# Gate and up of three row blocks in 64-row pairs on TensorE's own semaphore, two spectra kept, a third weight buffer

## The chip, the cores and the metric

The kernel runs on one NeuronCore of one Trainium2 chip. The metric is the device time of one execution in microseconds. Five engines take part: TensorE (PE; its weight loads are listed apart as PEld), VectorE (DVE), ScalarE (ACT), GpSimd (POOL) and SyncE (SP), which issues nearly all transfers. Each works through its own queue in order; semaphores tie the queues together.

## The reference

One transformer layer on 2048 rows of 576 channels: a long convolution with a gate, then a gated feed-forward part, each behind a layernorm that a condition vector scales and shifts.

```python
sa, ca, ga, sb, cb, gb = six rows of (silu(c) @ w_mod)
h = layernorm(x) * (1 + ca) + sa
kv = (4-tap causal shift of k by shift_k) * v
y = causal convolution of kv with ssm_k over 2048 steps (by FFT, per channel) + kv * ssm_D
x = x + ga * (h * y)
h = layernorm(x) * (1 + cb) + sb
x = x + gb * ((silu(h @ w1) * (h @ w3)) @ w2)        # w1, w3: 576 x 4608, w2: 4608 x 576
```

Inputs and output are bf16.

## The kernel before

**Two strands of work.** The feed-forward part runs over four row blocks `r` of 512 rows (`RB`). For each, *gate and up* computes 36 hidden tiles `f` of 128 columns of `h @ w1` and `h @ w3`, and `down` (L1043) multiplies the hidden 512 x 4608 block by `w2` in two column halves of nine chunks each. Beside it runs the convolution of the next two 256-row blocks `s0`, `s1`, written as a Python generator (`conv`, L822) whose steps each state a cost. After every hidden tile, `hide` (L964) calls `advance` (L903), which adds an allowance to `due` and takes steps until their costs have used it up. The allowance is `rate * 2.05`, times `HEAD_PACE` (1.8) for the first eight tiles of `r` > 0; `down` gives one per chunk. So a convolution step's matmuls enter TensorE's queue among those of the feed-forward part. On the other engines a compile-time scheduler orders what is ready by program order; `behind` and `issue_after` fix an order by hand. In `down`, after six chunks of the second half, `end` takes all steps left, and `turn_all` (L793) transposes the last rows for the next row block.

**The convolution.** Block `s` of `k*v` and of the filter become spectra `X[s]` and `V[s]` (six 128 x 576 planes each). `forward2` (L310) makes one with four pairs of 288-column matmuls into PSUM and a ScalarE copy of each. `pair` (L408) multiplies an X with a V and adds to the block's sum `z`: two DVE instructions over 3456 elements. `inverse` (L544) transforms `z` back. Three X and four V fit in SBUF; the others are written to DRAM (`keep_x`, `keep_v`) and read again (`get`, L440). `outcome` (L751) does the steps from `z` to the normalised rows `h2row`; `ln_sums` (L448) takes two ScalarE passes for a layernorm's sums. `k_rows` (L363) transposes the filter rows.

**Gate and up.** A hidden tile contracts 576 channels: four 128-row tiles and one of 64 rows. Its gate and up sums fill the two banks of one of four PSUM buffers (`ps`, L72). For `r` < 3, `stream` (L914) takes two tiles at a time: 128-row matmuls (`full`, L943), then the 64-row remainders (`rest`, L954), gate on array rows 0 to 63 and up on rows 64 to 127, then 128-row matmuls again. For `r` = 3, `stream_halves` (L1004) uses 64-row matmuls alone. They come in pairs on the upper and lower array rows, one into each bank: five pairs (`part(f, 0)`), then four (`part(f, 1)`) with the banks swapped. [...] A one-element POOL memset on `tok` waits for the first part's last matmul, and the swapped part's first matmul waits for the memset:

```python
for f in range(NF + 1):
    if f < NF:
        ...
        part(f, 0)
    if f > 0:
        part(f - 1, 1)
        hide(f - 1)
```

The 36 tiles' weights come in nine jobs of four tiles. `load_w13` (L894) puts 1152 KB into one of the buffers `wst[0]`, `wst[1]` by turns. `wst[2]` is the same memory as `w2m`, which holds four chunks of `w2` for `down`.

Of the kernel before, what the change touches and what calls it, by code (L numbers as in the profile page):

```python
# [33 lines left out]
SPLIT = 2  # L34
HEAD = 8
HEAD_PACE = 1.8
# [10 lines left out]
class _Kernel:  # L47
    def __init__(self, ctx, tc, q, k, v, shift_k, ssm_k, ssm_D, w1, w3, w2, c, w_mod, out):
# [21 lines left out]
        self.gets = 0  # L70

# [4 lines left out]
    def setup(self):  # L76
# [3 lines left out]
        self.tok = const.tile([1, 1], F32, name="tok")  # L80
# [215 lines left out]
    def forward(self, basis, rhs, dst):  # L296

        nc = self.nc
        for e in range(2):
            for cs in range(2):  # L300
                ps = self.ps()
                for cc in range(2):
                    for h in range(2):
                        nc.tensor.matmul(ps[:, h, 0:H], basis[:, cc * (e + 1), cs],
                                         rhs[:, cc, h * H:(h + 1) * H],
                                         start=(cc == 0), stop=(cc == 1))
                nc.scalar.copy(dst(e, cs).rearrange("p (h d) -> p h d", h=2), ps[:, :, 0:H])
                yield -1.0

    def forward2(self, basis, rhs, both, odd, diff):  # L310
# [3 lines left out]
        for cc, dst in ((0, both), (1, odd)):  # L314
            for cs in range(2):
                ps = self.ps()
                for h in range(2):
                    nc.tensor.matmul(ps[:, h, 0:H], basis[:, cc, cs], rhs[:, cc, h * H:(h + 1) * H],  # L318
                                     start=True, stop=True)
                nc.scalar.copy(dst[:, cs].rearrange("p (h d) -> p h d", h=2), ps[:, :, 0:H])  # L320
                yield -1.9
# [34 lines left out]
    def x_sums(self, s):  # L356
        X = self.X[s]
        self.nc.vector.tensor_add(X[:, 0:6:3, :], X[:, 1:6:3, :], X[:, 2:6:3, :])
        if 3 < s < NBLK - 2:
            self.keep_x(s)  # L360
        yield 0.75

    def k_rows(self, s):  # L363
# [5 lines left out]
        for cc in range(2):  # L369
            for ct in range(5):  # L370
                nc.tensor.transpose(pt[:, cc, ct * P:(ct + 1) * P], nat[:, ct, cc:B:2],
                                    self.ident[:])
        nc.scalar.copy(kT[:], pt[:, :, 0:D])
# [59 lines left out]
    def old_x(self, i, s):  # L433

        return self.X[i] if s == 2 or s == 4 and i > 0 else self.get("X", i)
# [12 lines left out]
    def ln_sums(self, src, i, ssum, ssq, col=None):  # L448
        col = i if col is None else col
        for func, scale, out in ((ACT.Copy, -1.0 / D, ssum), (ACT.Square, D ** -0.5, ssq)):  # L450
            junk = self.lnp.tile([P, D], BF16, name="junk", tag="junk")
            self.nc.scalar.activation(junk[:], src[:, i, :], func, scale=scale, accum_out=out[:, col:col + 1])  # L452
# [40 lines left out]
    def gate_stats(self, s):  # L493

        ssum, ssq = [self.small.tile([P, 2], F32, name="l1" + k, tag=t) for k, t in (("s", "ssum"), ("q", "ssq"))]
        for i in range(2):
            with self.behind(self.nc.scalar):
                self.ln_sums(self.xo[s], i, ssum, ssq)
            yield 0.8
# [44 lines left out]
    def inverse(self, s, cc):  # L544
        nc = self.nc
        z = self.accs[s]
        ps = self.ps()
# [4 lines left out]
        for i, (b, cs, row) in enumerate(terms):  # L552
            for h in range(2):
                nc.tensor.matmul(ps[:, h, 0:H], self.Fb[:, b, cs], z[:, row, h * H:(h + 1) * H],
                                 start=(i == 0), stop=(i == len(terms) - 1))
        return ps
# [27 lines left out]
    def turn(self, pt, cc):  # L584
        for ct in range(5):
            self.nc.tensor.transpose(pt[:, cc, ct * P:(ct + 1) * P],  # L586
                                     self.h2row[:, cc, ct * P:(ct + 1) * P], self.ident[:])
# [20 lines left out]
    def turned(self, s, pt, c0, n):  # L608
# [4 lines left out]
        for ct in range(5):  # L613
            dst = hT[:, ct, t * P:(t + n) * P].rearrange("p (c t) -> p c t", c=n)
            src = pt[:, c0:c0 + n, ct * P:(ct + 1) * P]
# [27 lines left out]
    def first_block(self):  # L643
# [54 lines left out]
        self.ln_sums(x1, 0, sums[0], sums[1], 0)  # L698
# [7 lines left out]
        ps = [self.inverse(0, cc) for cc in range(2)]  # L706
# [44 lines left out]
    def outcome(self, s, fill, waits, between=None, quick=False):  # L751


        def steps():
# [4 lines left out]
            for cc in range(2):  # L759
                nc.scalar.copy(y[:, cc, :].rearrange("p (h d) -> p h d", h=2), self.inverse(s, cc)[:, :, 0:H])  # L760
# [13 lines left out]
            else:  # L774
                sums = [self.small.tile([P, 2], F32, name="l2" + k, tag=t) for k, t in (("s", "ssum"), ("q", "ssq"))]
                for i in range(2):
                    with self.behind(nc.scalar):
                        self.ln_sums(self.xo[s], i, *sums)
                    yield 0.0
# [42 lines left out]
    def conv(self, s0):  # L822
# [13 lines left out]
        def old():  # L836
            V, X = self.old_v(s0 - 1, s0), self.old_x(1, s0)
            yield from self.pair(X, V, s0, s0 == 2)
            for j in range(2, s0):
                X = self.old_x(j, s0)  # L840
                yield from self.pair(X, V, s1)
                V = self.old_v(s0 - j, s0)
                yield from self.pair(X, V, s0)
            self.V1 = V
# [8 lines left out]
        def beside():  # L853
# [7 lines left out]
            self.X1 = self.old_x(1, s0)  # L861
# [12 lines left out]
        def others():  # L874
            yield from self.kv_rows(s1)
            self.gate_shift(s1)
            yield from self.mix(self.x_spectrum(s1), more())
            yield from self.x_sums(s1)
        yield from self.outcome(s0, others(), (5.0, 4.5, 6.0, 0.0), lambda: self.gate_rows(s1))
# [23 lines left out]
    def advance(self, cost):  # L903

        self.due += cost
        while self.due > 0 and self.steps is not None:
            c = next(self.steps, None)
            if c is None:
                self.steps = None
                break  # L910
            self.due -= c
# [85 lines left out]
    def wait_for(self, later, first):  # L997

        self.tc.add_manual_dep(
            later, first.name,  # L1000
            mybir.DependencyInfo(mybir.DependencyClass.Sync, mybir.DependencyReason.DATA),
            reason="both halves of the rows write this bank, one after the other")

    def stream_halves(self, r):  # L1004
# [3 lines left out]
        newest = lambda: nc.cur_bb.bb.instructions[-1]  # L1008
        gus, ws, marks = {}, {}, {}

        def part(f, swap):
            w = ws[f // FC]
            cols = slice(f % FC * P, (f % FC + 1) * P)
            for ct in range(4 if swap else 5):
                for rows, i in ((slice(0, 64), swap), (slice(64, P), 1 - swap)):
                    nc.tensor.matmul(gus[f][:, i, :], w[rows, 5 * i + ct if ct < 4 else 4, cols], hT[rows, ct, :],  # L1016
# [180 lines left out]
```

## Time and profile before

| what | us |
|---|---|
| median of 3 runs (519.62 to 520.41) | 520.09 |
| the profiled execution | 519.61 |
| its span, first to last instruction | 517.8 |
| `r` = 0 with the start, to 171.6 | 171.6 |
| `r` = 1: gate and up / down | 82.8 / 37.8 |
| `r` = 2: gate and up / down | 79.1 / 37.3 |
| `r` = 3: gate and up / down and end | 70.1 / 39.1 |
| PE / DVE / ACT busy | 498.4 / 345.5 / 292.9 |

The stage borders are read from the chain of work that ended last. The profile page lists busy time by engine, the chain, groups of instructions with the idle time before them and what ended it, and transfers. A timeline gives instructions in order of time. The end of a matmul is modelled, so its starts are the safer reading.

### The profile page before, as it was taken

The page shows a single profiled execution, that of the slowest core. Times are in us where ns is not written, and L with a number is a line of the kernel's source. Part 1 is how long each engine was busy: PE and PEld are TensorE (multiplying, and loading weights), DVE is VectorE, ACT ScalarE, POOL GpSimd, SP SyncE. Part 2 cuts the span into 40 slices and gives each one's busy share as a digit, 9 for nine tenths or more (in the row PEclk, how much of TensorE's full clock was granted, in tenths as well). Part 3 has the DMA queues.
Part 4 walks back from the last instruction along what each step waited for, and adds up shares of the span by engine and source line. Part 5 has one row for each costly group of instructions (what it writes and reads, how often), then busy time and mean ns, then how long its engine had stood idle before and what let it go on. Part 6 is the DMA issues. An engine that isn't in the chain of part 4 may idle for free.

```text
span 517.8 us, 9255 instructions
## 1 busy us (share of the span) xinstructions
PE 498.4 (96%) x3650; PEld 294.8 (57%) x3650; DVE 345.5 (67%) x557; ACT 292.9 (57%) x581; POOL 26.1 (5%) x75
## 2 busy tenths in 40 slices
PE   7999989889989999899999999999999999999997
PEld 3667765456868544343677644434587644444775
DVE  8888799999997287989999637998711222221012
ACT  5748689649254488577641467958651355555000
POOL 3100000000000001000001000000100000000000
PEclk9999999989999999999999999999999999999999
DMA  8947959646998696688788549653655535532462
GB/s 262 331 151 210 308 178 289 203 143 221 315 342 270 207 312 230 214 284 289 230 270 280 161 147 361 200 173 91 184 147 151 161 107 176 175 110 77 117 181 69
DMA packets 102207, 107.80 MB, mean 208 GB/s; under 512 B 5075, under 2 KB 94228, under 8 KB 102164
## 3 DMA queue, kind: packets, MB, share of 16 engines
q1 hardware_dynamic: 102142, 107.21, 66.5%
q8 instruction: 28, 0.46, 0.4%
q14 instruction: 15, 0.12, 0.1%
q10 hardware_dynamic: 22, 0.01, 0.0%
HBM read 96.00 MB, written 11.21 MB: 207 GB/s over the span
## 4 chain that ended last, share of the span: by engine, by line
PE 70%; DVE 20%; DMA 4%; ACT 3%; issue 2%; POOL 1%; SPq 0%; DVEq 0%; POOLq 0%; ACTq 0%
PE ps L949 24%; PE ps L1061 22%; PE ps L1016 14%; PE ps L960 4%; DVE p L420 3%; DMA wst<-in_B_w_dram 3%; DVE z L422 3%; DVE h L971 2%; PE ps L318 2%; DVE z L414 1%; DVE kv L342 1%; DVE kvt L341 1%; PE ps L253 1%; DMA knat<-in_A_ssm_k_dram 1%; ACT junk L452 1%
## 5 line engine op out<-in xcount | busy, mean ns | idle before, releaser
L949 PE MATMUL ps<-h2T,wst 128*128 128x512 bf16 (+1 forms) x1056 | 201.1, 341 | 1.9 <-DMA wst<-in_B_w_dram 0.9
L949 PEld LDWEIGHTS <-wst 128*128 128x128 bf16 x1056 | 100.3, 98 | 87.7 <-issue 14.8
L1061 PE MATMUL ps<-wst,h 128*128 128x288 bf16 x1152 | 145.1, 286 | 2.4 <-DVE og L1078 1.4
L1061 PEld LDWEIGHTS <-h 128*128 128x128 bf16 x1152 | 112.3, 98 | 32.0 <-issue 3.1
L968 ACT ACTIVATE h<-ps 128x512 bf16<-128x512 f32 x108 | 65.2, 603 | 64.7 <-PE ps L960 40.8
L1016 PE MATMUL ps<-h2T,wst 64*128 64x512 bf16 x648 | 70.1, 376 | 0.0
L970 ACT CAST u<-ps 128x512 bf16<-128x512 f32 x108 | 63.7, 590 | 0.0
L971 DVE TENSOR_TENSOR h<-h,u 128x512 bf16<-128x512 bf16 x108 | 44.5, 417 | 24.6 <-ACT u L970 24.6
L420 DVE TENSOR_TENSOR p<-X,V 128x3456 bf16<-128x3456 bf16 x28 | 54.6, 1951 | 2.0 <-DMA X<-Xd 1.8
L422 DVE TENSOR_TENSOR z<-z,p 128x3456 bf16<-128x3456 bf16 x28 | 54.6, 1950 | 0.2
L1016 PEld LDWEIGHTS <-wst 64*128 64x128 bf16 x648 | 31.5, 94 | 38.4 <-DMA wst<-in_B_w_dram 0.4
L1031 DVE TENSOR_TENSOR h<-h,u 128x512 bf16<-128x512 bf16 x36 | 15.3, 425 | 54.9 <-ACT u L1030 54.9
L1078 DVE TENSOR_TENSOR og<-ps,gbrow 128x288 bf16<-128x288 f32 x32 | 13.1, 449 | 50.5 <-PE ps L1061 50.5
L1028 ACT ACTIVATE h<-ps 128x512 bf16<-128x512 f32 x36 | 21.5, 598 | 36.2 <-PE ps L1016 36.2
L452 ACT ACTIVATE junk<-x 128x576 bf16<-128x576 bf16 x54 | 37.1, 687 | 0.5
L616 ACT ACTIVATE h2T<-ps,sbcol,cbcol 128x256 bf16<-128x256 bf16 x35 | 16.7, 569 | 34.6 <-PE ps L586 34.6
L960 PE MATMUL ps<-h2T,wst 64*128 64x512 bf16 (+1 forms) x264 | 32.9, 341 | 0.0
L581 ACT ACTIVATE h2row<-x,l2n,l2r 128x576 bf16<-128x576 bf16 (+1 forms) x24 | 14.0, 660 | 13.4 <-DVE l2n L466 13.4
L1030 ACT CAST u<-ps 128x512 bf16<-128x512 f32 x36 | 20.9, 581 | 0.0
L960 PEld LDWEIGHTS <-wst 64*128 64x128 bf16 x264 | 8.5, 94 | 21.0 <-issue 19.9
L341 DVE TENSOR_TENSOR kvt<-kh,shk 128x1152 bf16<-128x1152 bf16 x24 | 18.1, 752 | 0.9 <-DMA kh<-in_A_k_dram 0.6
L342 DVE TENSOR_TENSOR kv<-kv,kvt 128x1152 bf16<-128x1152 bf16 x24 | 18.1, 754 | 0.4
(140 smaller groups left out, 389.5 us busy)
## 6 DMA issues: line engine op xcount, KB each, us to landing
wst<-in_B_w_dram SPq DMA_DIRECT2D x80, 512.0 KB, 4.3
wst<-in_B_w_dram SPq DMA_DIRECT2D x72, 288.0 KB, 3.6
X<-Xd SPq DMA_DIRECT2D x8, 864.0 KB, 7.1
Xd<-X SPq DMA_DIRECT2D x6, 864.0 KB, 5.2
wst<-in_B_w_dram SPq DMA_DIRECT2D x80, 64.0 KB, 3.3
kh<-in_A_k_dram SPq DMA_DIRECT2D x7, 720.0 KB, 6.4
Vd<-V SPq DMA_DIRECT2D x4, 864.0 KB, 8.1
V<-Vd SPq DMA_DIRECT2D x4, 864.0 KB, 6.4
```

The lines of the kernel that those rows point to most:

```text
L341: nc.vector.tensor_mul(tmp[:], kh[:, 3 - j:5 - j, :], tap(j))
L342: nc.vector.tensor_add(kv[:], kv[:], tmp[:])
L420: nc.vector.tensor_mul(p[:], X[:], V[:])
L422: nc.vector.tensor_add(z[:], z[:], p[:])
L452: self.nc.scalar.activation(junk[:], src[:, i, :], func, scale=scale, accum_out=out[:, col:col + 1])
L949: nc.tensor.matmul(gus[k][:, i, a * n:(a + 1) * n], w[:, 5 * i + ct, (fi + a) * P:(fi + a + 1) * P], hT[:, ct, t0:t1], start=(first and ct ...
L960: nc.tensor.matmul(gus[k][:, i, a * n:(a + 1) * n], w[rows, 4, (fi + a) * P:(fi + a + 1) * P], hT[rows, 4, t0:t1], start=(first and a == 0 ...
L968: nc.scalar.activation(h3, gus[k][:, 0, :].rearrange("p (a t) -> p a t", a=m), ACT.Silu)
L970: nc.scalar.copy(u[:], gus[k][:, 1, :])
L971: nc.vector.tensor_mul(h3, h3, u[:].rearrange("p (a t) -> p a t", a=m))
L1016: nc.tensor.matmul(gus[f][:, i, :], w[rows, 5 * i + ct if ct < 4 else 4, cols], hT[rows, ct, :], start=swap == 0 and ct == 0, stop=swap == ...
L1061: nc.tensor.matmul(acc[t], self.h3[:, f0 + f, t * P:(t + 1) * P], w[:, f, :], start=(f0 + f == 0), stop=(f0 + f == NF - 1))
```

## The change

- **64-row pairs for `r` = 1, 2 and 3.** `stream_halves` replaces `stream` there and takes the convolution's steps too. While it runs, `halves` is set. The matmuls of `forward2`, `forward` and `inverse` go through `two_banks`, which issues a first part in 64-row pairs, yields, and issues the swapped part later (`close`). `k_rows` and `turn` use 64-row transposes into two banks, `k_rows` with two copies on ScalarE in place of one.
- **TensorE's own semaphore.** The POOL memset is gone. `after` puts a TensorE nop that waits for the first part's last matmul, and the swapped part is queued behind the nop. Between the two lie `AHEAD` = 2 of the next tile's five pairs.
- **Third buffer.** From `r` = 1 on the nine jobs use buffers 0, 1, 2, 0, 1, 2, 0, 1, 0.
- **Spectra kept.** `X[4]` and `X[5]` are neither written to DRAM nor read back: two stores and two loads of 864 KB fewer. For `s0` = 6 the sums run in another order, so one V more is read and four X instead of six: X loads fall from eight to five, V loads rise from four to five.
- **Spread steps.** `advance` is called twice per tile with `rate * 1.02`, takes 5 units at most in one call, and stops behind a first part or a layernorm pass (`pause`). `HEAD_PACE` is 1.4. `ln_sums` yields 0.4 after each pass, which adds 1.6 units to each `outcome`. For `s0` = 2 the inverse comes after 9 units of other steps instead of 5. One product of the second block's sum is moved ahead of `x_spectrum(s1)`.

```diff
-HEAD_PACE = 1.8
+AHEAD = 2
+HEAD_PACE = 1.4
+    def after(self, first):
+        with self.behind(self.nc.tensor):
+            nop = self.nc.tensor.nop().ins
+            self.tc.add_manual_dep(nop, first.name, <sync, data>, ...)
+        return self.tc.issue_after(nop)
+
+    def two_banks(self, outs, terms):
+        mm = self.nc.tensor.matmul
+        if not self.halves:
+            for n, term in enumerate(terms):
+                for i in range(2):
+                    mm(outs[i], *term(i, slice(0, P)), start=(n == 0), stop=(n == len(terms) - 1))
+            return
+        for swap in range(2):
+            with self.after(mark) if swap else nullcontext():
+                for n, term in enumerate(terms):
+                    for rows, i in ((slice(0, 64), swap), (slice(64, P), 1 - swap)):
+                        mm(outs[i], *term(i, rows), start=(swap == 0 and n == 0),
+                           stop=(swap == 1 and n == len(terms) - 1))
+            if swap == 0:
+                mark = self.newest()
+                self.pause = self.open = True
+                yield 0.0
...
     def x_sums(self, s):
-        if 3 < s < NBLK - 2:
-            self.keep_x(s)
...
     def k_rows(self, s):
+        if self.halves:
+            for cc in range(2):
+                for ct in range(5):
+                    for half in range(2 if ct < 4 else 1):
+                        rows, at = slice(64 * half, 64 * half + 64), 320 * cc + 64 * ct
+                        nc.tensor.transpose(pt[:, half, at:at + 64], nat[rows, ct, cc:B:2],
+                                            self.ident[rows, rows])
...
     def old_x(self, i, s):
-        return self.X[i] if s == 2 or s == 4 and i > 0 else self.get("X", i)
+        return self.X[i] if s == 2 or s == 4 and i > 0 or i >= 4 else self.get("X", i)
...
     def ln_sums(self, src, i, ssum, ssq, col=None):
-            self.nc.scalar.activation(junk[:], src[:, i, :], func, scale=scale, accum_out=out[:, col:col + 1])
+            with self.behind(self.nc.scalar):
+                self.nc.scalar.activation(junk[:], src[:, i, :], func, scale=scale, accum_out=out[:, col:col + 1])
+            self.pause = self.halves or func == ACT.Square
+            yield 0.4
...
+                V, X = self.old_v(1, s0), self.old_x(s0 - 1, s0)
+                yield from self.pair(X, V, s0)
+                for j in range(2, s0):
+                    V = self.old_v(j, s0)
+                    yield from self.pair(X, V, s1)
+                    X = self.old_x(s0 - j, s0)
+                    yield from self.pair(X, V, s0)
+                self.X1 = X
...
-            yield from self.mix(self.x_spectrum(s1), more())
+            rest = more()
+            yield next(rest)
+            yield from self.mix(self.x_spectrum(s1), rest)
...
-        yield from self.outcome(s0, others(), (5.0, 4.5, 6.0, 0.0), lambda: self.gate_rows(s1))
+        yield from self.outcome(s0, others(), (9.0 if s0 == 2 else 5.0, 4.5, 6.0, 0.0), lambda: self.gate_rows(s1))
...
     def advance(self, cost):
         self.due += cost
-        while self.due > 0 and self.steps is not None:
+        left = self.due - 5.0
+        while self.due > max(left, 0.0) and self.steps is not None:
...
+            if self.pause:
+                self.pause = False
+                break
+
+    def close(self):
+        if self.open:
+            self.open = False
+            c = next(self.steps)
+            self.due -= c
+            self.spent += c
...
-    def stream_halves(self, r):
+    def stream_halves(self, r, jobs, rate):
+        def part(k, swap, some=slice(None)):
+            (fc, _, _, _, _), fi = items[k]
+            cols = slice(fi * P, (fi + 1) * P)
+            order = (0, 1, 2, 3) if swap else (4, 0, 1, 2, 3)
+            for ct in order[some]:
...
+        self.halves = True
+        begin(0)
+        for k in range(len(items)):
+            mark = part(k, 0, slice(AHEAD, None))
+            self.close()
+            self.advance(rate * 1.02 * (HEAD_PACE if k < HEAD else 1.0))
+            begin(k + 1)
+            self.close()
+            with self.after(mark):
+                part(k, 1)
+            hide(k)
+            self.advance(rate * 1.02 * (HEAD_PACE if k < HEAD else 1.0))
+        self.halves = False
...
+                bufs = [b if b == 2 else (r + b) % 2 for b in (0, 1, 2, 0, 1, 2, 0, 1, 0)]
+                jobs = [(fc, 0, RB, bufs[fc], (lambda f, i: lambda: f(i))(*spills[fc]) if fc in spills else None)
...
-            if r == NRB - 1:
-                self.stream_halves(r)
+            if r > 0:
+                self.stream_halves(r, jobs, rate)
```

`begin(k)` fetches the job's weights, takes a PSUM buffer and issues the first two pairs of tile `k`; behind the last tile it does nothing. The loop over convolution blocks 2 and 4 keeps its old order.

## The prediction

> **What bounds the kernel now.** I read the shares of busy time first, then the chain of work that ended last in order of time, then busy time by stage, then the waits and TensorE's timeline for what lies inside the stages.
>
> ```profile
> PE 498.4 (96%) x3650; PEld 294.8 (57%) x3650; DVE 345.5 (67%) x557; ACT 292.9 (57%) x581; POOL 26.1 (5%) x75
> ```
>
> TensorE is busy for 96% of the span, so only TensorE time counts, or the waits between. The chain says where it is TensorE's own pace:
>
> ```profile
> 153.94 0.74 DVE og L1078 x2
> 154.72 10.45 PE ps L1061 x84
> ...
> 304.23 3.56 PE ps L949 x16
> 308.33 3.56 PE ps L949 x16
> 312.42 3.56 PE ps L949 x16
> ...
> 408.64 70.03 PE ps L1016 x648
> ```
>
> Up to 154 the chain runs mostly through VectorE (r = 0 is balanced between the two); from 171 it is nearly all TensorE. The three L949 rows start 4.10 and 4.09 us apart: two hidden tiles in `stream`. The last row is all of r = 3 in 64-row pairs: 70.03 / 36 = 1.945 us a tile, 3.89 for two, and 1.945 / 9 = 0.216 for a pair. Both forms stream the same columns, so `stream` loses 0.21 us in two tiles. The waits name the loss:
>
> ```profile
> PEld L960 <- issue: 19.9, 52, 0.4
> PEld L949 <- issue: 14.8, 38, 0.9
> ```
>
> Each time the array goes from 128-row to 64-row matmuls or back, the weight load idles 0.4 us with nothing to wait for; two such turns lie in two tiles, so a turn costs TensorE 0.105 net. Then the stages (columns: window, length, busy time of PE, PEld, DVE, ACT, POOL, clock, DMA share, GB/s) and TensorE's real gaps, in brackets:
>
> ```profile
> 171.60:254.40 82.80, 80.56 (x426) 33.94 (x424) 67.48 (x102) 61.01 (x122) 2.07 (x3) 1.00 0.79 255
> 292.20:371.30 79.10, 78.59 (x405) 32.41 (x403) 60.99 (x96) 58.55 (x118) 4.58 (x3) 1.00 0.59 188
> ```
>
> ```profile
> 105.56 1.12 PE L554 MATMUL ps<-z,Fb 128*128 128x288 bf16 x4 [3.72 <-DVE z L540]
> 219.80 0.41 PE L318 MATMUL ps<-kv,Fb 128*128 128x288 bf16 x2 [1.35 <-DVE kv L344]
> 244.92 1.04 PE L949 MATMUL ps<-h2T,wst 128*128 128x512 bf16 x4 [0.90 <-DMA wst<-in_B_w_dram]
> ```
>
> Gate and up of r = 1 is thus 18 x 4.10 = 73.8 of streaming, 2.2 idle and 6.8 of convolution matmuls; r = 2 is 73.8, 0.5 and 4.8.
>
> [...]
>
> **The change part by part**, against the profiled span of 517.8.
>
> *Fewer turns.* r = 1 and 2 lose 18 x 0.21 = 3.8 us each: **-7.6**. Transforms between tiles are 64-row too, so they bring no turns back. r = 3 had none.
>
> *The new wait.* The trace has no TensorE nop waiting for TensorE. Nearest rows: in r = 3 a matmul that starts at 421.10 releases the ScalarE activation at 421.52, so completion is visible 0.42 after the start. A VectorE result that ended at 105.41 started TensorE's weight load at 105.53 and matmul at 105.56: of that 0.15, 0.04 is the hop already counted, 0.11 the restart. Together 0.53. The cover is the mark's own pair and two of the next tile, 3 x 0.216 = 0.65, so 0.12 is to spare: **0** for 105 tiles. Behind the last tile `begin` issues nothing, and 0.53 - 0.22 = 0.31 shows, three times: **+0.9**. Bounds: 0, if something later fills it; with the cover gone, 0.31 on all 108 tiles, +33. [...] POOL's 36 memsets (3.2 us busy) never held anything up: nothing gained.
>
> *Transforms in 64-row pairs.* Each 128-row matmul becomes two 64-row ones that run side by side, 288 columns as before: 0. `k_rows` goes from 10 transposes in 0.67 us to nine pairs and a bit, each bounded by a 0.094 weight load, some 0.9; three of them: **+0.7** (0 to +2, if paired loads go one by one). The second ScalarE copy of `kT` copies the same columns: some 0.2, hidden (ScalarE 61 of 82.8 busy; against some 78 it is 78%).
>
> *PSUM.* A transform now holds its buffer across its two parts. `begin(k+1)` needs one of four, 0.86 us (four pairs) after the previous tile's last pair starts. That tile's own buffer comes free after 0.42 + 0.61 + 0.60 = 1.6. If two transforms are open, it must be that one, and TensorE waits 0.75. The two stages have about 35 transforms of 1.9 cost units, a tile gets about 2.1, so two open is rare. I take **+1.0**; bounds 0 and, at a third of them, +9.
>
> *Transfers.* The third buffer gives a load two jobs of 8 us instead of one; the 0.90 gap goes: **-0.9** (0 to -1.5). The price: `w2`'s first four chunks can no longer wait in `wst[2]` from the end of the previous `down`; they start after job 5, 12 tiles = 23 us before they are read, against 3.6 us each: hidden. Job 2 must wait for the previous `down` to end, SP holds what is queued behind it (filter rows, k, v and q for the next blocks), then has 8 tiles, 16 us. Two stores and two loads less free DMA time, which the path does not feel: 0. The new order needs V[3] when its slot has only just come free, 6.4 us for VectorE; early in r = 2 VectorE ran little but the hidden tiles from 293 to 314, so it is hidden.
>
> *Spread steps, r = 1 and 2.* `HEAD_PACE` 1.4 moves 8 x 0.4 x 2.04 = 6.5 units times a rate of 1.04 to 1.16, so 7 units, behind; the two `outcome`s add 3. `x_spectrum(s1)` comes some 6 us later on TensorE while VectorE goes on, so the 1.35 gap should go; a like one of 0.51 at 347.9 may stay: **-0.9** (-1.9 to +2). The tail moves as well. Before, `inverse(5)` stood at 253, its `h2row` was done at 278.4 and the transposes came at 285.6: 7.2 to spare. Some 10 units later at 2.1 a chunk (2.0 us) is 9.5 us, and r = 1 may wait 2 at `turn_all`. In r = 2, `h2row` was done at 391.7 for 402.0: enough. **+1.0** (0 to +8).
>
> *r = 0.* The 9 units and the spread aim at gaps: 3.72 + 0.22 at the inverse, 0.59 + 0.72 + 0.39 around 71 to 78. But VectorE works without a break from 107 to 123, with short ones to 161, and sets two later points: the eviction at 153.94, for which TensorE already waited 1.41, and `h2row(3)` at 164.1, which TensorE read at 165.0. TensorE would come earlier and wait there: **-0.5** (-6.8 if VectorE's order moves too, +2 if the added units delay `h2row`).
>
> Sum: -7.6 + 0.9 + 0.7 + 1.0 - 0.9 - 0.9 + 1.0 - 0.5 = -6.3, a span of 511.5. The median of 520.09 lies 2.3 above the span (the profiled execution, 519.61, lies 1.8 above it), so **513.8 us**.
>
> **Rivals.**
>
> *B, r = 0 gives up its gaps too.* For it: 5.6 us of TensorE gaps lie before 110, plus 1.4 at 154. Against it: VectorE's unbroken row. With 6 more: 508.
>
> *C, the tail hands the gain back.* The rows reach `turn_all` late in r = 1 and 2, and TensorE waits 2 to 3 us more in each. For it: 7.2 to spare against 9.5 of shift. Against it: VectorE may finish sooner, as its queue in `down` was filled with products of the next blocks. 518.5.
>
> *D, slower: the nop's wait is not covered.* Place: before each swapped part. From 0.07 us a tile beyond the 0.12 to spare it eats the 7.6 (7.6 / 108). At 0.2 a tile, +21.6: 535. For it: no such wait is in the trace and the margin is thin. Against it: the parts of the path, each measured, fit.
>
> *E, no difference.* PSUM waits at the third of transforms, +8 more: about 520.
>
> **How the numbers follow.** Chances: my forecast 0.48 (its own range 510.5 to 517), B 0.20, C 0.14, D 0.13, E 0.05. A measurement tells 0.2%, 1.0 us, from no change. Faster: 0.48 + 0.20 + most of C = 0.78; same: a bit of C, and half of E, 0.05; slower: D and the rest, 0.17. The range 507 to 521 holds the forecast, B, C and E, and leaves D out.
>
> **What would show it.** In the profile after: no idle for issue at gate-and-up weight loads from 172 on; r = 1 at some 78.5 us, r = 2 at 76.3, r = 3 still 70 to 70.5; the two half-parts a tile at 0.216 a pair with no gap at the nop; the 0.90 gap gone; X loads five, V loads five. I am wrong if a tile of r = 3 takes over 1.97 us (D), if TensorE waits for ScalarE at a tile's first pair, if the transposes of `turn_all` wait for `h2row` (C), or if r = 0 ends well before or after 171.

## The result, and the profile after

The changed kernel takes 538.96 us (median of 4 runs, 536.58 to 542.45) against 519.86 us for the kernel before (4 runs, 519.60 to 520.41): a ratio of 1.037, 95% interval 1.031 to 1.043. It is 19 us slower where 6 us faster was forecast, and outside the range. Its profiled execution took 538.41 us with a span of 536.4, which is 18.6 more than the span of 517.8 before.

The shares of busy time and TensorE's slices, from the page of the changed kernel:

```profile
PE 498.4 (93%) x4302; PEld 312.2 (58%) x4306; DVE 346.4 (65%) x557; ACT 296.2 (55%) x583; POOL 23.6 (4%) x39
...
PEclk9999999989999999979999899998999999999999
```

No engine has much more to do (TensorE is busy for 498.4 us in both), so the 18.6 us are time in which TensorE stands; the account below adds what a slower clock costs. The stages show where (same columns as before: window, length, busy PE, PEld, DVE, ACT, POOL, clock, DMA share, GB/s):

```profile
172.60:259.90 87.30, 77.70 (x733) 41.79 (x733) 58.45 (x93) 59.56 (x118) 2.07 (x3) 0.96 0.59 197
304.30:389.30 85.00, 78.85 (x704) 40.56 (x704) 61.83 (x93) 57.31 (x114) 2.07 (x3) 0.95 0.57 182
```

Gate and up of `r` = 1 took 82.8 us before and 87.3 now, of `r` = 2 79.1 and 85.0; the `down` of `r` = 1 37.8 and 44.4. `r` = 0 (+1.0), the `down` of `r` = 2 (+0.1), `r` = 3 (+0.3) and the end (+0.2) hardly moved. Of the 6.6 us that the `down` of `r` = 1 is longer, 3.3 are TensorE work of the convolution that came later than before (40.7 us busy instead of 37.4), and 2.9 are a gap at its end. Two rows of the chain of work show that the pairs run as they should wherever nothing stops them:

```profile
316.86 22.23 PE ps L1087 x206
...
426.71 69.17 PE ps L1087 x640
```

That is 103 pairs in `r` = 2 and 320 in `r` = 3, each 0.216 us, across the TensorE waits between the parts. But in `r` = 1 the same chain leaves TensorE for 50 us. From 181.90 to 231.29 it runs almost only over a transfer, VectorE and ScalarE, where it was mostly gate-and-up matmuls before:

```profile
181.90 0.65 SPq L966
182.59 5.49 DMA kh<-in_A_k_dram
188.10 0.76 DVE kvt L372
...
193.95 1.96 DVE p L460
196.24 1.87 DVE z L462
...
222.23 1.88 DVE p L460
224.13 1.96 DVE z L462
226.42 1.88 DVE p L460
228.32 1.96 DVE z L462
230.65 0.59 ACT u L1110
231.29 0.43 PE ps L1087
```

The timeline of the changed kernel around 227 us tells how a hidden tile gets caught in this. First VectorE, then ScalarE, then TensorE; in brackets the idle time before, and what ended it:

```profile
221.81 0.42 DVE L1111 TENSOR_TENSOR h<-h,u 128x512 bf16<-128x512 bf16 x1
222.15 1.95 DVE L460 TENSOR_TENSOR p<-X,V 128x3456 bf16<-128x3456 bf16 x1
224.13 1.96 DVE L462 TENSOR_TENSOR z<-z,p 128x3456 bf16<-128x3456 bf16 x1
226.00 0.42 DVE L1111 TENSOR_TENSOR h<-h,u 128x512 bf16<-128x512 bf16 x1
...
230.20 1.76 DVE L1111 TENSOR_TENSOR h<-h,u 128x512 bf16<-128x512 bf16 x5
```

```profile
226.46 0.58 ACT L1110 CAST u<-ps 128x512 bf16<-128x512 f32 x1 [3.11 <-DVE h L1111]
...
230.65 0.59 ACT L1110 CAST u<-ps 128x512 bf16<-128x512 f32 x1 [3.11 <-DVE h L1111]
```

```profile
227.09 0.42 PE L99 MATMUL ps<-z,Fb 64*128 64x288 bf16 x4 [2.61 <-ACT u L1110]
231.29 0.58 PE L1087 MATMUL ps<-h2T,wst 64*128 64x512 bf16 x1 [3.78 <-ACT u L1110]
...
246.53 0.61 PE L1087 MATMUL ps<-h2T,wst 64*128 64x512 bf16 x4 [2.14 <-ACT u L1110]
```

A hidden tile needs one product `h` of VectorE (0.42 us), which frees a `u` buffer. TensorE could deliver a tile every 1.95 us, but here two convolution instructions stand before each product, so there is one product in 4.2 us. Product by product, the delay behind the end of its `u` copy grows to 13.5 us; before it was never above 4.5. Then all four `u` buffers are full, ScalarE's copy of the next tile's up sums waits, the PSUM buffer stays taken, and TensorE stops. The waits of the changed kernel (total us, times, longest) have the whole row of them:

```profile
ACT u L1110 <- DVE h L1111: 15.2, 10, 3.1
PE ps L1087 <- ACT u L1110: 11.1, 6, 3.8
DVE kvt L372 <- DMA kh<-in_A_k_dram: 11.0, 2, 7.0
...
PE ps L99 <- ACT u L1110: 3.8, 3, 2.6
...
PE ps L1087 <- DVE og L1161: 2.9, 1, 2.9
```

Before, ScalarE never waited for the product and TensorE waited 0.4 us in all for `u`; VectorE's wait for `kh` was 0.6. The last line is the gap at the end of the `down` of `r` = 1. Another PSUM buffer stays taken there: VectorE reads the sums of `down` (`og`) at 303.44, behind a row of products and additions that fills its queue from 289.60 on.

The clock is the second part. The trace's clock record has TensorE at half speed from 228.25 for 6.83 us, from 303.34 for 6.83 and from 368.20 for 3.41, in each case at or behind gaps of 2.6 to 3.8 us. Before, the only such stretch ahead of the end (3.41 us) came with the 3.72 gap in `r` = 0.

**An account of `r` = 1 and 2.** For each kernel I took the time from the last `w2` product of `r` = 0 to the last of `r` = 2, both row blocks with their `down`. Gaps are distances between the starts of successive TensorE matmuls above 0.6 us, less 0.22 each. The clock's loss is half of the half-speed time outside the gaps: from 228.25 to 235.08 a pair takes 0.427 us in the median, instead of 0.216. The rest is what TensorE needs when nothing holds it. Each row comes from the one profiled execution of its kernel.

| kernel | us | gaps | clock | rest |
|---|---|---|---|---|
| before | 237.0 | 3.5 | 0 | 233.5 |
| after | 254.0 | 19.4 | 6.5 | 228.1 |

So the pairs did save 5.4 us, and 15.9 us of new gaps with 6.5 us of lost clock came on top: +17.0 of the +18.6. Of the 19.4 us of gaps, 15.3 end with `u` and 2.9 with `og`. The experiments are read with the same account.

### The profile page after: what moved, and what is told of

The parts are those of the page before. It is cut to its first block, busy times and chain, and to the rows that moved or that the text cites. A ratio compares the mean times of both kernels' runs of the same rounds, so it can differ in the third digit from the quotient of the medians.

```text
span 536.4 us, 10464 instructions
## 1 busy us (share of the span) xinstructions
PE 498.4 (93%) x4302; PEld 312.2 (58%) x4306; DVE 346.4 (65%) x557; ACT 296.2 (55%) x583; POOL 23.6 (4%) x39
## 4 chain that ended last, share of the span: by engine, by line
PE 55%; DVE 24%; ACT 9%; DMA 7%; issue 2%; POOL 1%; SPq 1%; POOLq 0%; DVEq 0%; ACTq 0%
PE ps L1087 26%; PE ps L1144 18%; PE ps L1026 6%; DVE z L462 5%; DMA wst<-in_B_w_dram 5%; DVE p L460 5%; ACT junk L493 3%; PE ps L93 2%; DVE kv L373 1%; DVE kvt L372 1%; ACT u L1110 1%; DVE h L1111 1%; ACT h L1108 1%; DMA kh<-in_A_k_dram 1%; DMA V<-Vd 1%
## 5 line engine op out<-in xcount | busy, mean ns | idle before, releaser
L1087 PE MATMUL ps<-h2T,wst 64*128 64x512 bf16 x1944 | 224.7, 383 | 14.8 <-ACT u L1110 11.1
L1087 PEld LDWEIGHTS <-wst 64*128 64x128 bf16 x1944 | 106.3, 95 | 112.2 <-issue 16.0
L1111 DVE TENSOR_TENSOR h<-h,u 128x512 bf16<-128x512 bf16 x108 | 44.1, 421 | 76.7 <-ACT u L1110 76.6
L1026 PE MATMUL ps<-h2T,wst 128*128 128x256 bf16 (+1 forms) x477 | 69.0, 296 | 2.7 <-DMA wst<-in_B_w_dram 2.2
L1110 ACT CAST u<-ps 128x512 bf16<-128x512 f32 x108 | 63.0, 583 | 15.2 <-DVE h L1111 15.2
L1026 PEld LDWEIGHTS <-wst 128*128 128x128 bf16 x480 | 46.2, 99 | 21.1 <-issue 3.8
L462 DVE TENSOR_TENSOR z<-z,p 128x3456 bf16<-128x3456 bf16 x28 | 54.7, 1952 | 0.3
L664 ACT ACTIVATE h2T<-ps,sbcol,cbcol 128x256 bf16<-128x256 bf16 x35 | 16.7, 570 | 14.9 <-PE ps L626 14.9
L351 ACT CAST X<-ps 128x576 bf16<-128x576 f32 x24 | 15.7, 653 | 5.8 <-PE ps L93 5.1
L812 ACT CAST y<-ps 128x576 bf16<-128x576 f32 x14 | 8.6, 644 | 17.7 <-PE ps L93 16.9
L503 POOL TENSOR_TENSOR l2r<-l2v,neghalf 128x2 f32<-128x2 f32 x6 | 8.2, 1364 | 214.0 <-DVE l2v L502 214.0
```

The costliest lines, as they stand in the source:

```text
L462: nc.vector.tensor_add(z[:], z[:], p[:])
L1026: nc.tensor.matmul(gus[k][:, i, a * n:(a + 1) * n], w[:, 5 * i + ct, (fi + a) * P:(fi + a + 1) * P], hT[:, ct, t0:t1], start=(first and ct ...
L1087: nc.tensor.matmul(gus[k][:, i, :], ws[fc][rows, 5 * i + ct if ct < 4 else 4, cols], hT[rows, ct, :], start=swap == 0 and ct == 4, stop=sw ...
L1110: nc.scalar.copy(u[:], gus.pop(k)[:, 1, :])
L1111: nc.vector.tensor_mul(h3, h3, u[:])
```

## The experiments

Each `us` is the median of at least 4 runs. Ratios are to the kernel before, run on the same chip.

### Which part of the change carries the loss

128-row matmuls (`stream`) for `r` = 1 and 2, all else as changed:

```diff
-            if r > 0:
+            if r == NRB - 1:
                 self.stream_halves(r, jobs, rate)
```

> The changed kernel with 128-row tiles again in r = 1 and 2; 64-row pairs and the nop on TensorE's semaphore stay in r = 3, and the kept spectra, the third buffer and the spread steps stay everywhere. My first theory: VectorE falls behind in r = 1 and 2 (its queue waits for k rows and for X from DRAM, with the hidden tiles' products queued behind), ScalarE's u then finds no free buffer, PSUM does not come free, TensorE stands still for 2 to 4 us at a time and its clock halves for 3.4 or 6.8 us after each. If the transfers and the step order make VectorE late, this is still slow, 530 or more. If the pairs in r = 1 and 2 are what brings the wait onto TensorE, it is 518 to 523. The rival that the nop's wait is uncovered expects r = 3 above 72 us; I expect 70.4.

Measured: 524.5 us, ratio 1.007 (1.004 to 1.011). The pairs of `r` = 1 and 2 cost 14.5 of the 19 us. In the account, this kernel's two row blocks take 236.8 us like those before (gaps 2.6, clock 0, rest 234.3). In its profile the other 5 us lie ahead of them: `r` = 0 ended at 176.0 instead of 171.3. It ended at 172.4 in the changed kernel, so within the two row blocks the pairs cost 17.2 us. Why `r` = 0 was longer here was not followed up.

The pairs alone, with two weight buffers, no kept spectra and the old steps:

```diff
-                bufs = [b if b == 2 else (r + b) % 2 for b in (0, 1, 2, 0, 1, 2, 0, 1, 0)]
+                bufs = [(r + fc) % 2 for fc in range(NF // FC)]
-HEAD_PACE = 1.4
+HEAD_PACE = 1.8
...
```

> Of the whole change the 64-row pairs alone (gate, up and transforms from row 512 on): two w1/w3 buffers, no kept spectra and the steps of before. Theory 1: the loss is there with the pairs alone, 538 to 550 us (third buffer missing, which was worth 7 us, steps not spread, worth 3). Rival (the loss comes from how the parts meet, above all from the third buffer's earlier loads or from the spread steps): 525 or less.

Measured: 540.8 us, 1.040 (1.034 to 1.046). The pairs bring the loss with them (gaps 25.0, clock 4.2, rest 228.7). But with two buffers it isn't all VectorE's: TensorE waits 12.9 us for weights, beside 9.2 for `u`.

The other parts, one undone at a time. The spectra:

```diff
-        return self.X[i] if s == 2 or s == 4 and i > 0 or i >= 4 else self.get("X", i)
+        return self.X[i] if s == 2 or s == 4 and i > 0 else self.get("X", i)
...
+        if 3 < s < NBLK - 2:
+            self.keep_x(s)
```

> The changed kernel with X[4] and X[5] written out and read back, and the sums of s0 = 6 in the order of before. If the new order's wait for V and X (VectorE waits 4.5 and 1.3 us for X in r = 2, and SyncE holds the weights 14.6 us behind a V load that has no slot) costs most, this gains 8 us or more, down to about 530. If the lateness comes from r = 1's step order, it gains under 4 us.

Measured: 539.73 us, 1.036 (1.031 to 1.041): no difference. The third buffer (the `bufs` lines above):

> The changed kernel with two weight buffers by turns, wst[2] free for w2. If the third buffer's loads push the k rows back in SyncE's queue and take w2's lead (TensorE waits 0.97, 0.62, 0.76 us for weights in down), this gains 3 us or more. If not, it is within 2 us of the changed kernel's 539.

Measured: 546.39 us, 1.050 (1.045 to 1.054), 7 us more than the whole change. The waits of this kernel:

```profile
PE ps L1087 <- DMA wst<-in_B_w_dram: 15.4, 4, 11.9
```

With pairs and two buffers TensorE waits 15.4 us for weights, where the kernel before waited 0.9 in gate and up. The spread steps (`HEAD_PACE` 1.8, no limit in `advance`, no yields in `ln_sums`, the old `outcome` and `x_spectrum(s1)`):

> The changed kernel with the step order of before: HEAD_PACE 1.8, no limit of 5 units, no cost and no pause for the layernorm passes, 5 units before the inverse of s0 = 2, the product of s1 behind again. Advance is still called twice a tile, and a first part still ends a call. If the later pace makes VectorE late, this gains 8 us or more (to about 530 or below); if VectorE is late from its loads alone, it is 535 to 543.

Measured: 541.84 us, 1.041 (1.036 to 1.047), 3 us more, though the intervals overlap; in the account the two row blocks take 5.3 us more. So none of these parts makes the loss. The third buffer reduces it, and less surely so do the spread steps. A slower pace of the steps, `rate * 0.918` for `rate * 1.02`:

> The changed kernel with the steps' allowance in gate and up of r = 1 and 2 cut by a tenth (0.918 for 1.02 twice a tile), so that more of the convolution falls into down. If VectorE is given more per tile than a tile lasts, this gains 5 us or more (534 or less). If VectorE's lateness comes from single waits for loads or spectra, it is within 4 us of 539.

Measured: 542.11 us, 1.041 (1.036 to 1.045): handing the steps out a tenth slower does not help.

### Is it VectorE's work?

Leave out the additions of the products of blocks 4 to 7 (22 of 28, 1.95 us each), once in the changed kernel and once in the kernel before:

```diff
         yield 2.0
-        nc.vector.tensor_add(z[:], z[:], p[:])
+        if s < 4:
+            nc.vector.tensor_add(z[:], z[:], p[:])
```

> The changed kernel without the additions z = z + p of convolution blocks 4 to 7 (the kernel leaves that part of the sums out). It takes 18 or so VectorE instructions of 1.95 us out of r = 1 and 2 and changes nothing else on TensorE, ScalarE or the queues. If VectorE is too late with the hidden tiles' products, and that is what stops ScalarE and TensorE, the TensorE gaps of r = 1 and 2 and the half clock go and the time falls by 15 us or more, to about 512 to 524. If the gaps come from ScalarE's own queue or from PSUM held by open transforms, it falls by under 5.

> The kernel before without the same additions (that part of the sums is left out here too). VectorE is not what bounds r = 1 and 2 there, so I expect 516 to 519. With e5 it gives what the change is worth when VectorE is not short: if e5 lies below this by 3 or more, the fewer turns of the array are a real gain; if e5 is above it, they are not.

Measured: 520.31 us in the changed kernel (1.000, 0.998 to 1.003) and 518.81 in the one before (0.998, 0.996 to 0.999). The same relief is worth 18.7 us with pairs and 1.3 without. The waits of the changed kernel with less VectorE:

```profile
ACT u L1111 <- DVE h L1112: 5.5, 5, 1.4
...
PE ps L1088 <- ACT u L1111: 4.1, 5, 2.1
```

Gaps fall from 19.4 to 6.0, the clock's loss from 6.5 to 1.4; the rest stays (227.8). So TensorE's side of the forecast was right, and VectorE's work is what most of the gaps waited for. Gate and up take 78.8 and 77.0 us, near the 78.5 and 76.3 that the prediction had, but that is in part luck: 2.8 us of TensorE's convolution work moved to the `down` of `r` = 1, and some gaps remain.

By the test that was written down for these two runs, the change is no gain even here: the changed kernel stays 1.5 us above the other, at the edge of the noise. In the account it is 235.2 us against 236.0 (gaps 2.2, clock 0, rest 233.8). Of the 6.0 us that TensorE needs less, the gaps and the clock that remain take all but 0.8.

Give the product `h` to GpSimd for `r` < 3, so that it no longer queues on VectorE:

```diff
-            nc.vector.tensor_mul(h3, h3, u[:])
+            (nc.gpsimd if r < NRB - 1 else nc.vector).tensor_mul(h3, h3, u[:])
```

> The changed kernel with the hidden tiles' product h = h * u of r = 1 and 2 on GpSimd, which has little to do, so that it stands in no queue behind the convolution. If VectorE's queue is the cause, TensorE's waits for u go and it is 520 or less, provided that GpSimd needs under 1.9 us for one product; if it needs more, it is the bound and the time is above 540. If PSUM held by open transforms is the cause, it stays at 535 to 542.

Measured: 557.93 us, 1.071 (1.066 to 1.075). By its expectation (520 or less if a product takes under 1.9 us) this counts against the queue. But the groups of this kernel, and a wait, show that VectorE's own work changed too:

```profile
L1111 POOL TENSOR_TENSOR h<-h,u 128x512 bf16<-128x512 bf16 x72 | 114.7, 1606 | 86.3 <-ACT u L1110 86.0
...
L462 DVE TENSOR_TENSOR z<-z,p 128x3456 bf16<-128x3456 bf16 x28 | 62.7, 2240 | 0.5
```

```profile
PE ps L99 <- DVE z L581: 15.3, 2, 8.1
```

A product takes 1606 ns in the mean instead of 421. VectorE's additions of 3456 elements go from 1952 to 2240 ns in the mean: the nine of 28 that ran beside a product took 2.79 to 2.90 us, the others 1.95 to 1.96. ScalarE's wait for the product fell from 15.2 to 0.3 us and TensorE's for `u` from 14.9 to 5.4, so the first link was gone; but TensorE now waited 15.3 us for the convolution's `z`. What freeing the product alone is worth, this run can't tell.

### Is it the order of VectorE's queue?

VectorE was idle for 28.8 of the 87.3 us of `r` = 1, and its queue is fixed at compile time. Between two products it holds up to some 5 us of convolution work in the changed kernel and then none for several tiles. Before, and in the kernel with `stream`, it mostly holds about 2. I suspected that the compile-time scheduler spaces tiles of 64-row matmuls too wide, which was not tested. My first explanation was therefore this order alone. First I held the convolution's VectorE work behind the product of the last tile but one (then the last tile):

```diff
+            muls.append(nc.vector.tensor_mul(h3, h3, u[:]).ins)
...
+        def steps(cost=None):
+            with self.tc.issue_after(muls[-2]) if len(muls) >= 2 else nullcontext():
+                self.close() if cost is None else self.advance(cost)
```

> The whole change, with one thing added: each convolution instruction that VectorE gets while gate and up run in halves is kept, in VectorE's queue alone, behind the product h of the last tile but one that stands ahead of it in the program. No work is added or left out; 0 to 4 us of other VectorE work then stand between two products, 2.4 us in the mean, in place of stretches of 3.5 to 5.4 us and stretches of nothing. Theory 1 (the order of VectorE's queue makes the product late, and with it u, the bank and TensorE): the gaps before the pairs on u's copy go from some 18 us to under 5, the half clock after them goes too, r=1 and r=2 come to 78 to 81 us each and the time to 516 to 525. Theory 2 (VectorE simply has too much between the tiles, or the pairs themselves hold TensorE back by their waits): the gaps stay, the time is 534 or more. Theory 3 (held-back convolution work keeps the transforms waiting instead): u's waits go but TensorE waits for z, kv or X, 528 to 540.

> As the run before, but behind the last product that stands ahead in the program, so that VectorE's queue has program order. Theory 1: the same time within 4 us, 514 to 525, or a little more where work that was ready waits for a product. Theory 2: 534 or more. Theory 3: 4 us or more above the looser hold.

> The looser hold, with the first eight tiles of a row block getting the same allowance of convolution work as the others (factor 1.0 in place of 1.4), so that 0 to 4 us stand between products from the first on. Theory 1: within 3 us of the looser hold, faster by 1 to 2 us if the first tiles' heavier share still makes products late. Theories 2 and 3: no difference from the looser hold beyond 2 us.

Measured: 556.16 us (1.068, 1.060 to 1.075), 569.37 (1.094, 1.088 to 1.099) and 557.69 (1.071, 1.065 to 1.077). The third case of the expectation came, at a higher price. TensorE's waits for `u` fell from 14.9 to 6.2 us with the looser hold, but it waits for `kv` instead: the stage of `r` = 2, and TensorE's longest wait, of which 15.3 us lie in that stage,

```profile
304.00:406.20 102.20, 81.99 (x723) 39.47 (x722) 88.84 (x113) 57.51 (x114) 5.71 (x3) 0.90 0.50 166
```

```profile
PE ps L99 <- DVE kv L375: 24.6, 4, 10.8
```

The hold also forbids VectorE to do a row block's first convolution work in the `down` before it. From 120 us to the end of `r` = 0 VectorE has 27.8 us of work instead of 46.4, and gate and up of `r` = 2 get 88.8 us instead of 61.8. So this run measures a full VectorE, not an even queue.

For a cleaner test VectorE's queue was written out as a list: the changed kernel's own order, with convolution work only moved back inside its row block, so that at most about 2.2 (or 2.6) us stand between products before the next one is let through.

```diff
+    def hold_vector(self):
+        block = [i for i in self.nc.cur_bb.bb.instructions if i.engine == self.nc.vector.engine]
+        ...
+        for a, b in zip(ORDER, ORDER[1:]):
+            self.tc.add_manual_dep(block[b], block[a].name, <no sync, data>, ...)
```

> The whole change with VectorE's queue written out as a list: the changed kernel's own order, in which convolution work is moved back behind later products of the same row block wherever more than 2.2 us of it would stand between two products of row blocks 1 and 2. Nothing is moved forward, and what is not placed by the end of the row block's products follows them. The densest two tiles in a row have 6.2 us in place of 9.9. Theory 1 (VectorE's order makes products late, u's four buffers fill, the bank stays taken): the waits of TensorE for u halve at least, 522 to 531 us. Rival (the pairs themselves hold TensorE up, whatever VectorE's order): 534 to 543. Third case (delayed convolution work is missed by the transforms): TensorE waits for kv, z, X or V in place of u, 534 or more.

> The same with 2.6 us as the bound between two products. Theory 1: 522 to 533, within 4 us of the run before. Rival: 534 to 543.

The reverse puts the changed kernel's VectorE order, by such a list, into the kernel with `stream` in `r` = 1 and 2:

> The kernel with 128-row products in row blocks 1 and 2 (64-row pairs in row block 3 alone, third buffer, kept spectra and spread steps as in the change), which took 524.5 us, with VectorE's queue put by a list into exactly the order that it has in the whole change. Theory 1: its products come late by the same stretches of 3.5 to 5.4 us, r=1 and r=2 get gaps before gate and up on u's copy, and the time goes to 531 to 542. Rival (the order is harmless, the pairs do it): 522 to 527.

Measured: 536.43 us (1.031, 1.029 to 1.034), 534.36 (1.027, 1.025 to 1.030) and 527.73 (1.014, 1.011 to 1.018). Spreading won 2.5 us, within the noise, and 4.6; the bad order cost the 128-row kernel 3.2. In the account the three are 3.1, 3.5 and 5.7. All three runs lie between the theories' numbers or on the rival's side: this much of the order is worth some 3 to 6 us of the loss. My first explanation fell as the whole. The spreading was not complete: products still came up to 8.4 us late. In the spread kernel the waits for the product are nearly gone, but not TensorE's for `u`:

```profile
PE ps L99 <- ACT u L1110: 6.3, 2, 4.0
...
PE ps L1087 <- ACT u L1110: 2.9, 3, 2.1
...
ACT u L1110 <- DVE h L1111: 1.3, 1, 1.3
```

Its ScalarE timeline ahead of one of them, which ended at 239.43, shows the next link: the convolution's own chain.

```profile
235.33 1.63 ACT L556 ACTIVATE hg<-x,l1n,l1r 128x576 bf16<-128x576 bf16 x2 [1.86 <-DVE x L607]
236.86 0.67 ACT L493 ACTIVATE junk<-x 128x576 bf16<-128x576 bf16 x1
...
238.33 0.58 ACT L1108 ACTIVATE h<-ps 128x512 bf16<-128x512 f32 x1
```

ScalarE waits 1.86 us for a gated row of VectorE (`x`), then does 3.0 us of layernorm before it gets to the tile that has been waiting. The longest, which ended at 377.87, has the same shape, with a wait of 3.03 us. In this queue too, the hidden tiles stand behind a convolution that is late. In the account, the spread kernel (2.2) has gaps 16.0, clock 7.6, rest 227.3. The 128-row kernel with the bad order has gaps 8.3, no lost clock, rest 234.2. Its products came up to 13.0 us late, as in the changed kernel (13.5), yet TensorE lost 11 us less in gaps.

### The transforms in halves, or ScalarE?

Transforms in 128 rows again, so that none holds a PSUM buffer open, then the same with the queue spread:

```diff
-        if not self.halves:
+        if True:
             for n, term in enumerate(terms):
```

> The whole change, but the transforms of the convolution are 128-row matmuls again, written without a break; gate and up stay in pairs. So no open transform holds one of the four PSUM tiles across half a tile, and each transform costs two switches between the modes. Theory A (open transforms hold the banks): the gaps before pairs and transforms fall by half or more in r=1 and r=2, 520 to 530. Theory B (VectorE's and ScalarE's share of the convolution keeps its own pace, whatever form the transforms have): the gaps stay, the half clock after them too, 534 to 545.

> Transforms in 128 rows as in the run before and VectorE's queue spread to at most 2.6 us between two products. Theory A: 516 to 527. Theory B: the 3 to 5 us that spreading was worth come off the run before, 530 to 541.

Measured: 542.53 us (1.044, 1.042 to 1.045) and 539.64 (1.037, 1.034 to 1.040). The gaps stay (18.7 and 16.7): open transforms don't cause them. The rest rises from 228.1 to 231.2, so transforms in halves are worth about 3 us to TensorE.

Less of ScalarE's share:

```diff
+                w = 2 if self.halves else D
-                self.nc.scalar.activation(junk[:], src[:, i, :], func, scale=scale, accum_out=out[:, col:col + 1])
+                self.nc.scalar.activation(junk[:, 0:w], src[:, i, 0:w], func, scale=scale, accum_out=out[:, col:col + 1])
```

> The whole change; the sums and squares of the layer norms that ScalarE works out for the gated rows while gate and up run in halves (576 elements each) take 2 elements in place of 576: the statistics of these rows are left out in effect, some 0.5 us of ScalarE for each of them. The instructions, their order and their waits stay. Theory B: as with VectorE's share, a part of the gaps goes, 528 to 537. If only VectorE's lateness counts, or banks held by open transforms, no change: 537 to 542.

Measured: 534.11 us, 1.027 (1.025 to 1.029): 4.9 us won with 11.5 us of ScalarE time taken away, though ScalarE was busy for only 59.6 of 87.3 us. The account has gaps 14.7, clock 6.3, rest 227.8.

| kernel | us | gaps | clock | rest |
|---|---|---|---|---|
| after | 254.0 | 19.4 | 6.5 | 228.1 |
| 128 rows in `r` = 1, 2 | 236.8 | 2.6 | 0 | 234.3 |
| ... with the changed order of VectorE | 242.5 | 8.3 | 0 | 234.2 |
| less VectorE | 235.2 | 6.0 | 1.4 | 227.8 |
| less ScalarE | 248.8 | 14.7 | 6.3 | 227.8 |
| queue spread, 2.2 / 2.6 | 250.9 / 250.5 | 16.0 / 16.6 | 7.6 / 6.0 | 227.3 / 227.9 |
| transforms in 128 rows | 256.3 | 18.7 | 6.4 | 231.2 |

The last column is the same within 0.8 us for every kernel of this table whose gate, up and transforms run in pairs, and 6 higher for 128 rows. What differs is the gaps, and they follow the work of VectorE and ScalarE. No version that computes the whole layer was faster than the kernel before.

**What is shown, and what stays open.** Shown: the loss comes with the pairs; it is gaps and the clock behind them, not slower matmuls. Most of it goes when VectorE has less convolution work, and part of it when ScalarE has; some 3 to 6 us of it are the order of VectorE's queue. Argued, not shown: why the same VectorE work left room at 128 rows. A TensorE that needs 6 us less in two row blocks reaches each result sooner and then waits for it, which would account for some 6 of the 11 us of gaps between the changed kernel and the 128-row kernel in its order. A late `kh` (11.0 us of VectorE's waiting in the changed kernel, 2.9 with 128 rows) packs VectorE's work into what is left. It can't be the whole: with two weight buffers VectorE waits only 3.5 us for `kh`, and TensorE still 7.9 for `u`. How the remaining gaps divide between these stays open. So does whether it matters that `begin(k+1)` takes the next PSUM buffer before tile `k` has its swapped part, and what the order of ScalarE's queue is worth; neither was tried.

## Why the prediction was wrong

- **Fewer turns, -7.6, with the transposes' +0.7 and two of the three last tiles' +0.6: right, -6.3.** The rest of `r` = 1 and 2 fell by 5.4 against before, by 6.2 against 128 rows in the same kernel.
- **The new wait, covered: right.** `r` = 3 went from 70.1 to 70.4 us; the one uncovered tile was put at 0.31. A pair is 0.216 us across the waits, so rival D is refuted: the forecast ended on the wrong side for another reason than the one it named. That the swapped part needs its wait at all, and what a waiting nop holds up, were my assumptions, not shown: no run left the wait out.
- **PSUM, +1.0 (0 to +9): the step that failed.** It took a tile's buffer to come free a fixed 1.6 us after its last pair, 0.42 + 0.61 + 0.60, as if ScalarE always copied at once. It then looked for trouble only in open transforms, which the run with 128-row transforms rules out. What it left out is that the copy needs a `u` buffer, and this one needs VectorE's product; nor did it ask when VectorE would free the PSUM buffers of `down`. The numbers were there: VectorE was busy for 67.5 us of 82.8 in `r` = 1, which is 86% of the 78.5 forecast, and a share of a stage says nothing of its dense stretches. For `r` = 1 and 2 no term priced VectorE's order, which the new program would get from the scheduler. Measured: 15.9 us more of gaps and 6.5 of clock, past the bound of +9 and missing from every rival. The sign itself was in the list of what would show it wrong, TensorE waiting for ScalarE at a tile's first pair, but without a price.
- **Transfers, -0.9.** That keeping the spectra is worth nothing was right. The third buffer was worth 7 us, not 0.9: a quicker TensorE would have waited 15.4 us for weights with two. "Hidden" was wrong for what SP holds behind them: VectorE waited 11.0 us for `kh` instead of 0.6, and 3.5 with two buffers.
- **Spread steps, -0.9 + 1.0.** Without them some 3 us more, not clear of the noise. Rival C did not come: in the changed kernel, TensorE's only wait for `h2row` ahead of the transposes is 1.0 us.
- **`r` = 0, -0.5:** +1.0, within its bounds. The 3.72 us gap at the inverse became one of 4.46 at `kv` (109.25): moved, not closed.

The range failed with the likeliest case, since the case that came (a helper engine off the critical path that sets when PSUM comes free) was in none of the five.

## What to carry to other kernels

When TensorE is made quicker, follow each PSUM buffer to the last engine that must act before it is free, here ScalarE, then a small buffer, then VectorE, and compare the helper's densest stretch of queue, not its share of the stage, with the new tile time. The same cut of VectorE work was worth 1.3 us before the change and 18.7 after it, and even with it the quicker TensorE did not pay (520.31 us against 518.81). So try a lighter helper first, and only then a faster leader.

## What the runs showed of the hardware that was not expected

The clock costs a third as much again as the gaps do: 6.5 us beside 19.4. In the clock record of the changed kernel the half-speed stretches start at 108.78, 228.25, 303.34 and 368.20, which are 35, 22 and 19 times 3.413 us apart, and last 3.41 or 6.83 us. I divided TensorE's record in the traces of the kernels before and after at this spacing, laid on the half-speed stretches of each, from 14 us after the start to TensorE's last matmul (the ends of matmuls are modelled, so the idle times are a little rough). That gives 289 pieces of 3.413 us at full speed. All five in which TensorE stood for 1.97 us or more (1.97 to 3.41) were followed by half speed, and none of the other 284, with at most 1.76 us, was.

So the half speed goes with how much of a gap falls into one piece. The gap of 2.94 us that ended at 304.31 had 1.97 us in one piece and 0.96 in the next, and the clock was at half speed from 303.34. One of 2.14 us that ended at 246.53 had 0.93 and 1.21, and the clock stayed. The length of a gap does not decide it alone: one of 2.67 us that ended at 367.43 had 2.65 us in one piece, and 3.41 us at half speed followed, but the 128-row kernel with the changed order has a longer one (3.0 us of waiting for `u`, 3.36 between starts, at 371.34) and lost no clock in these row blocks.

A product of 128 x 512 took 1606 ns on GpSimd in the mean of 72 (GpSimd's times are rough), against 421 on VectorE. VectorE's own work in that kernel was slower too: the additions of 3456 elements took 2240 ns in the mean instead of 1952, and 2.79 to 2.90 us where a product ran beside them; the products of 3456 elements took 2105 ns instead of 1954. What made them longer was not tested.
